# Two heads' rows of an attention output moved into the padding of the other heads, ahead of its output product

## The chip, the cores and the metric

The kernel runs on one core of one Trainium2 chip. A core has engines that run at the same time, each in the order of its own queue: TensorE (PE: matmuls, with the loading of weights beside them as PEld), VectorE (DVE), ScalarE (ACT), GpSimd (POOL) and SyncE (SP, which here only issues transfers). They wait for each other by semaphores. Transfers between the chip's memory (HBM) and the on-chip memory (SBUF) are issued from a queue (SP, POOL or ACT) and land later. Matmuls write to eight banks of accumulators, which ACT or DVE must read out before a bank can be used again. The metric is the device time of one execution in microseconds (us), the median over runs.

## The reference

x has 2048 rows of D = 448. It is normalized (xn); one branch is a local attention with 16 heads of 28 dimensions, the other an MLP with F = 1792; the result is x + s * g.

```python
def _A_ref(x, wqkv, wo):                   # H = 16, Dh = 28, W = 8, dil = 2
    qkv = (x @ wqkv).reshape(B, S, 3, H, Dh) ...
    q, k, v = qkv[0], qkv[1], qkv[2]
    idx = pos[:, None] - off[None, :]      # a row sees itself and 7 rows, 2 apart
    ...
    attn = _softmax(logits, axis=-1)
    o = jnp.einsum("bhsw,bhswd->bhsd", attn, vg)
    return o.transpose(0, 2, 1, 3).reshape(B, S, D) @ wo

def _B_ref(x, w1, b1, w2, b2):
    h = _gelu(jnp.einsum("bsd,df->bsf", x, w1) + b1)
    return jnp.einsum("bsf,fd->bsd", h, w2) + b2

xn = _layernorm(x)
s = _A_ref(xn, A_wqkv, A_wo)
g = _silu(_B_ref(xn, B_w1, B_b1, B_w2, B_b2))
return x + s * g
```

## The kernel before

**Tiles and stages.** The even rows of x come first and the odd rows after them, so that the 8 rows that a query sees lie next to each other. The 2048 rows are 16 tiles of 128 (index t), four tiles to a chunk of 512 (index c). Per tile: statistics and `norm` (line 482) make xn, which is turned into xnT (D on the partitions, four groups kt of 128; the fourth holds the last 64 dimensions twice, on partitions 0 to 63 and 64 to 127). `qk_rows` (589) and `vproj` (612) make q, k and v; q and k are turned by transposing transfers into qkT, v goes through a buffer in HBM, v_hbm, and comes back per visit. `ff1` (665, L671 and the gelu L675) and `ff2` (691, L703) are the MLP; `gate` (732) makes g from it. Attention runs in nine visits of 228 (one of 224) queries: the scores (L770), exp on ACT (L779), the mask on DVE (L785), the values (L799), and then four steps on DVE (L808 to L822) that divide by the sum and write oT. `final` (853) multiplies oT with wo (L863; L871 for the last two tiles), and `gated` (877) multiplies by g (sg), adds x (o) and stores.

**Row tiling.** D = 448 is three and a half times 128. `pair` (534) therefore takes two tiles of rows at once and splits every product in two halves of 64 rows, which run side by side on the array: first tile a on partitions 0 to 63 and tile b on 64 to 127, for the kt in `before`, and then, after a *hop*, the other way round for the kt in `after`. With xn, whose fourth kt is there twice, that is 4 + 3 steps, 14 matmuls a pair. The hop (`told`, 550 to 554) is a wait on POOL's queue: POOL waits until the last matmul of the first part is done and tells TensorE, which holds the second part until then. Other pairs' matmuls are placed in between. A change between 128-row, 64-row and 32-row matmuls is a change of mode.

**oT and wo.** A head has 28 dimensions, but oT gives it 32 partitions: head 4g + l lies on partitions 32g to 32g + 27 of kt = l. The four partitions that are left, 28 to 31, 60 to 63, 92 to 95 and 124 to 127 in each kt, hold what the division makes of the sums, and wo has zeros there (the memset at line 370). So the final product takes all four kt in both halves: 4 + 4 steps, 16 matmuls for each pair (line 865).

**The order.** The kernel writes out no order by hand. Each step is a task with an engine, an assumed duration, tasks that it needs, and a priority (PRIO, LATER, NUDGE); `_Plan.run` (102) places them one after the other in an assumed time and emits every engine's queue in that order. In it, a transfer issued from POOL is assumed to take 0.45 us of the queue (`dma`, 372). The queues then run as the chip lets them.

Of the kernel before, what the change touches and what calls it, by code (L numbers as in the profile page):

```python
# [8 lines left out]
F32 = mybir.dt.float32  # L9
BF16 = mybir.dt.bfloat16  # L10
# [7 lines left out]
TILED = 30  # L18
BURST = 3.5
NUDGE = {  # L20
    61: 4, 64: -20, 140: -165, 160: -221, 163: -244, 165: -29, 397: 111, 413: -37, 490: 163, 669: -149,
}
LAST = 352
SAME = 20
# [154 lines left out]
def kernel(  # L179
# [37 lines left out]
    def tok(ap):  # L217
        return ap.rearrange("b (s two) d -> two (b s) d", two=2)

    x_half = tok(A_x)  # L220
    o_half = tok(out)

# [8 lines left out]
    def sb(name, shape, dt=BF16):  # L231
        return const.tile(shape, dt, name=name)
# [6 lines left out]
    w1 = sb("w1", [P, KT, F])  # L239
    w2 = sb("w2", [P, NMT, D])  # L240
    wo = sb("wo", [P, KT, D])
    b1r = sb("b1r", [P, P])
    b1 = sb("b1", [P, NMT], F32)
    b2 = sb("b2", [P, D])
    xnT = sb("xnT", [P, KT, S])
    qkT = sb("qkT", [P, 2, G, PAD + S])
    v_tok = [sb(f"v_tok{t}", [P, 2, H // 2, 32]) for t in range(4)]
    v_hbm = dram.tile([BACK + S, H * 32], BF16, name="v_hbm")
    oT = sb("oT", [P, KT, S])
    ident = sb("ident", [P, P])  # L250
    eps_t = sb("eps_t", [P, 1], F32)
    half_t = sb("half_t", [P, 4], F32)
# [9 lines left out]
    def ring(name, n, shape, dt=BF16, fifo=False):  # L262
        return _Pool([sb(f"{name}{i}", shape, dt) for i in range(n)], fifo)

    p_xn = ring("xn", 4, [P, 512])
    p_st = ring("st", 4, [P, 6], F32)
    p_E = ring("E", 8, [P, 512], fifo=True)
    p_dt = ring("dt", 2, [P, 512], F32)
    p_rd = ring("rd", 2, [P, H], F32)
    p_y = ring("y", 2, [P, D], F32)  # L270
    p_t = ring("t", 2, [P, D], F32)
# [13 lines left out]


    PRIO = {
        "project": (54, 6.5, -1, -796,),
        "project2": (-47, -24.5, -697.5, -972,),
        "values": (-60, -238.5, -708, -812.5,),  # L290
        "attn": (332.5, 150, 124.5, 209.5, 61, 182.5, 339.5, 196.5, 276,),
        "ff1": (75, 107.5, 161, -24.5, -31, 92, 171.5, -1, -8, 117.5, 54, 79.5, 64, 6.5, 40, 96.5,
            13.5, 22.5, -0.5, 30, 190, 161.5, 181, 165.5, 181, 129, 104, 64.5,),
        "gelu": (-8, 79.5, 28, 194.5,),
        "ff2": (91.5, -34.5, -96.5, 114.5, 129.5, 89, -831.5, 135, 120, 180.5, 59, 104, 147.5, 131,
            -12.5, -48,),
        "final": (207.5, 2, 71.5, -16.5, 55.5, -2, 174.5, 203, 37, 65.5, -16, 162.5, 87.5, 134, 36,
            -5,),
        "norm": (131, 11, 219.5, 294, 62, 220, -31, 168.5, 7, 29.5, 162.5, 183.5, -110, 4.5, 164,
            134,),  # L300
        "loads": (227.5, 186, 183, 40, 129.5, 100, 27, -66,),
        "stats": (49, 32, 205.5, 205.5, 112, 82, 130.5, -5, 44.5, 27, 147.5, 207.5, 114, 203.5,
            217, 161,),
        "turn_x": (198, 4.5, 200, 12.5, 259, 121, 98.5, 186.5, 57, 57, 72, 135.5, 79, 58, 135, 88,),
        "turn_qk": (18.5, 126, 116, 140, -16, 32.5, 118.5, -91.5, 79.5, 15, 161.5, 121.5, 77.5,
            162.5, 166, -17.5,),
        "move_v": (129.5, 145.5, 200.5, 147.5, 126, 210.5, 218.5, 150, 100.5,),
        "store_v": (103, 80.5, 21.5, 52, 191, 92, 149, 31, 118, 150, 333.5, -0.5, 106, 223.5, 214,
            111,),
        "spread": (-10.5, 75.5, 298, 99.5, 52.5, 186.5, 149.5, -55, 104,),  # L310
        "copies": (187, 4, 219, 15.5, 90, 177, 88.5, 31, 29, 20.5, 182, 51, 204.5, 49.5, 24,),
    }
    LATER = {"swap": 191.5, "qk": 27, "v": 148, "gelu": 32.5, "exp": 149.5, "mask": -4394.5, "pv": -29.5, "recip": 100, "os": 224, "y": 202, "tanh": 79.5, "g": 204, "sg": 165.5, "o": 222.5}

    plan = _Plan()

    def buf(pool, owner, i=0):
        return pool.bufs[owner.slots[pool][i]]

    def pe(n, k=1):  # L320
        return k * (n / 2400.0 + 0.0025)
# [14 lines left out]
    def memset(eng, ap, v):  # L336
        def fn(_):
            getattr(nc, eng).memset(ap, v)
        return fn
# [27 lines left out]
    t_head = plan.add("POOL", 0.6, mk_head, [t_on], prio=91)  # L367
    t_row0 = plan.add("POOL", 0.1, memset("gpsimd", row0[:], 0.0), [t_on], prio=93)
    t_row0 = plan.add("POOL", 0.1, memset("gpsimd", row0[:1, :], 1.0), [t_row0], prio=93)
    t_wo = [plan.add("POOL", 1.6, memset("gpsimd", wo[:], 0.0), [t_ident], prio=98)]  # L370

    def dma(eng, dst, src, kb, prio, deps=(), issue=0.45, rate=350.0, tail=1.7, share=0):
        def fn(_):
            i = {"SP": nc.sync, "ACT": nc.scalar, "POOL": nc.gpsimd}[eng].dma_start(dst, src)
# [96 lines left out]
    def half_bank(ap):  # L471
        return ap[:].bitcast(BF16)[:, :512].rearrange("p (a b) -> p a b", a=4)
# [377 lines left out]
        return []  # L850


    def final(t, prio):
        if t >= NT - 2:
            for i, (cs, n, end) in enumerate(parts(t)):
                if i:
                    ff2_part(t, cs, n, end, PRIO["ff2"][t], [last])
                last = final_part(t, cs, n, t_g[t][i], prio - 0.1 * i)
        elif t % 2 == 0:
            def job(t):  # L860
                def part(ps, kt, half, start, stop):
                    r = half_rows(half)
                    return nc.tensor.matmul(ps[:, :D], oT[r, kt, t * P:(t + 1) * P], wo[r, kt, :], start=start, stop=stop)  # L863
                return _Job(D, part, t_oT[t] + t_wo + [t_f2[t]], lambda u, own, i: gated(t, slice(0, D), D, t_g[t][0], u, own, i, prio))
            pair(job(t), job(t + 1), prio, False, (range(KT),), (range(KT),))

    def final_part(t, cs, n, g, prio):
        def f1(k):
            ps = buf(p_b, k)
            for kt in range(KT):  # L870
                nc.tensor.matmul(ps[:, :n], oT[:, kt, t * P:(t + 1) * P], wo[:, kt, cs],  # L871
                                 start=(kt == 0), stop=(kt == KT - 1))
        a = plan.add("PE", pe(n, KT), f1, t_oT[t] + t_wo + [t_f2[t]], prio, take=(p_b,), tail=0.15)
        gated(t, cs, n, g, a, a, 0, prio)
        return a

# [88 lines left out]


    def f_b1(k):
        nc.tensor.transpose(half_bank(buf(p_b, k))[:, 0, :], b1r[:], ident[:])
    b1_at = plan.add("PE", 0.06, f_b1, [t_b1r, t_ident], 345, take=(p_b,), tail=0.15)
    t_b1 = plan.add("DVE", 0.17, lambda _: nc.vector.tensor_copy(b1[:], half_bank(buf(p_b, b1_at))[:, 0, :NMT]), [b1_at], 90,  # L970
                    give=((p_b, b1_at, 0),))

# [7 lines left out]
    for i, (lo, hi) in enumerate(((0, 4), (4, 7), (7, 11), (11, 14))):  # L980
        t_w2[i // 2].append(dma("SP", w2[:, lo:hi, :], B_w2[lo * P:hi * P, :].rearrange("(m p) c -> p m c", p=P),
                                112 * (hi - lo), PRIO["loads"][4 + i], first, rate=230.0, share=hi - lo))
    t_b2 = dma("POOL", b2[:], B_b2.rearrange("(o d) -> o d", o=1).to_broadcast((P, D)), 112, 82, turned)
    t_wo += [dma("POOL", wo[32 * g:32 * g + 28, :, :], A_wo[112 * g:112 * g + 112, :].rearrange("(l c) d -> c l d", l=4),
                 100, 80, [t_w2[1][0]] + t_wo[:1]) for g in range(G)]
    for t in range(2 * TPC, NT):
        stats(t)
        if t % TPC == TPC - 1:
# [8 lines left out]
    for i, (c, what) in enumerate(STAGES):  # L997
        if what == "A":
            if was == "F":
                exps = []  # L1000
            run += blocks_of[c]
            if i + 1 == len(STAGES) or STAGES[i + 1][1] != "A":
                state["gate"], state["early"] = gels, gels[:-1]
                for what, b in visits(run):
                    exps += attn(b, what)
                run = []
        else:
            if was == "A":
                gels = []
            hs = [ff1(c, mt, PRIO["gelu"][c], exps) for mt in range(NMT)]  # L1010
            for i in range(0, NMT, 2):
                ff1_last[c] = pair(hs[i], hs[i + 1], PRIO["ff1"][7 * c + i // 2], c < 2)
            gels = gels + [t_h[(c, mt)] for mt in range(NMT)]
            if c == 0:
                project(2)
                project(3)
            for t in range(c * TPC, (c + 1) * TPC):
                ff2(t, PRIO["ff2"][t])
        was = what
    for t in range(NT):  # L1020
        final(t, PRIO["final"][t])

# [33 lines left out]
```

## Time and profile before

| | |
|---|---|
| median of 3 runs (lowest, highest) | 152.42 us (152.16, 152.49) |
| profiled execution: its own time | 152.14 us |
| profiled execution: span of the core | 150.4 us |
| granted TensorE clock | 0.998 |
| transfers on SP's queue (q1) | 37790 packets, 17.84 MB |
| transfers on POOL's queue (q0) | 512 packets, 1.18 MB |

The span runs from the first to the last instruction of the core; the time holds what lies around it too. In the groups of the profile a line such as L863 is the line of the kernel; "64*128 64x448" is a matmul on 64 rows and 128 columns of the array with 448 columns of data; "x112 | 12.6, 349" are 112 instructions that are busy for 12.6 us together, 349 ns each, so that two of them overlap.

### The profile page before, as it was taken

What the parts mean: (1) busy time and instruction counts of PE and PEld (TensorE: products, weight loads), DVE (VectorE), ACT (ScalarE), POOL (GpSimd) and SP (SyncE); (2) the same over time, 40 slices, a digit from 0 to 9 for tenths busy, and PEclk for the clock granted to TensorE, in tenths of its full rate; (3) what the DMA queues carried; (4) which work ended last, traced back from release to release, by engine and by line L of the source; (5) the groups of instructions that cost most, each with busy time, mean ns of one, the idle gap of its engine ahead of it and who ended that gap; (6) DMA issues with size and microseconds to landing.
All of it is one profiled execution on the core that took longest, in us unless ns stands there. A gap on an engine that the chain in (4) does not pass through costs nothing.

```text
span 150.4 us, 5216 instructions
## 1 busy us (share of the span) xinstructions
PE 146.1 (97%) x2173; PEld 76.9 (51%) x2173; DVE 113.7 (76%) x276; ACT 96.0 (64%) x168; POOL 18.4 (12%) x51
## 2 busy tenths in 40 slices
PE   7999999999999999999999999999999999999990
PEld 2644444544455555558556554445556445555460
DVE  3876850495546889899997989497998978995962
ACT  3365877658496594785788648888567497822020
POOL 7425530201750000011000000000000000000000
PEclk9999999999999999999999999999999999999999
DMA  4999869889999957159967994521120000001212
GB/s 155 327 314 362 126 124 159 261 119 361 185 161 197 72 100 139 37 114 226 125 201 175 147 256 128 125 74 38 36 65 7 0 0 4 4 0 61 63 63 63
DMA packets 38470, 19.47 MB, mean 129 GB/s; under 512 B 24887, under 2 KB 37758, under 8 KB 38446
## 3 DMA queue, kind: packets, MB, share of 16 engines
q1 hardware_dynamic: 37790, 17.84, 53.9%
q0 software_dynamic: 512, 1.18, 4.5%
q8 instruction: 17, 0.28, 0.8%
q10 hardware_dynamic: 144, 0.11, 0.2%
q14 instruction: 7, 0.06, 0.1%
HBM read 9.42 MB, written 3.94 MB: 89 GB/s over the span
## 4 chain that ended last, share of the span: by engine, by line
PE 97%; DVE 0%; ACT 0%; issue 0%
PE bank L671 28%; PE bank L703 25%; PE bank L595 14%; PE bank L618 7%; PE bank L863 7%; PE bank L799 4%; PE bank L725 4%; PE bank L346 3%; PE bank L770 3%; PE bank L871 1%; PE bank L519 1%; DVE sg L883 0%; ACT w_in L744 0%; PE bank L503 0%; DVE o L890 0%; PE bank L723 0%
## 5 line engine op out<-in xcount | busy, mean ns | idle before, releaser
L671 PE MATMUL bank<-xnT,w 64*128 64x512 bf16 x392 | 44.1, 376 | 0.0
L675 ACT ACTIVATE h<-bank,b 128x512 bf16<-128x512 f32 x56 | 34.5, 687 | 11.7 <-PE bank L671 11.5
L703 PE MATMUL bank<-w,h 64*128 64x448 bf16 x392 | 40.2, 349 | 0.0
L671 PEld LDWEIGHTS <-w 64*128 64x128 bf16 x392 | 18.8, 94 | 22.1
L703 PEld LDWEIGHTS <-h 64*128 64x128 bf16 x392 | 18.6, 94 | 16.8
L595 PE MATMUL bank<-w_in,xnT 64*128 64x448 bf16 (+1 forms) x212 | 24.8, 350 | 0.0
L779 ACT ACTIVATE E<-bank 128x456 bf16<-128x456 f32 (+1 forms) x36 | 16.9, 554 | 9.9 <-PE bank L770 8.6
L331 ACT CAST qk_tok<-bank 128x448 bf16<-128x448 f32 x25 | 12.3, 539 | 5.9 <-PE bank L595 4.8
L595 PEld LDWEIGHTS <-xnT 64*128 64x128 bf16 (+1 forms) x212 | 10.8, 94 | 9.4 <-DVE xnT L333 0.2
L808 DVE STREAM_TRANSPOSE dt<-bank 128x480 f32<-128x480 f32 (+1 forms) x18 | 12.1, 673 | 4.5 <-PE bank L799 4.5
L618 PE MATMUL bank<-w_in,xnT 64*128 64x448 bf16 (+1 forms) x106 | 14.0, 350 | 0.0
L863 PE MATMUL bank<-wo,oT 64*128 64x448 bf16 x112 | 12.6, 349 | 0.0
L817 DVE STREAM_TRANSPOSE dt<-rd 128x480 f32<-128x480 f32 (+1 forms) x18 | 12.1, 675 | 0.6
L822 DVE TENSOR_TENSOR oT<-bank,dt 128x456 bf16<-128x456 f32 (+1 forms) x18 | 11.4, 632 | 0.6
L785 DVE TENSOR_TENSOR E<-E,m_gen 128x456 bf16<-128x456 bf16 (+1 forms) x32 | 10.8, 390 | 0.0
L443 DVE BATCH_NORM_STATS2 st<-x_sb 128x6 f32<-128x448 bf16 x16 | 9.5, 606 | 1.7 <-DMA x_sb<-in_A_x_dram 1.7
L333 DVE CAST qk_tok<-bank 128x448 bf16<-128x448 f32 x7 | 4.3, 620 | 8.6 <-PE bank L595 8.6
L737 DVE TENSOR_TENSOR y<-bank,b 128x448 f32<-128x448 f32 x15 | 8.7, 619 | 1.9 <-PE bank L703 1.8
L749 ACT ACTIVATE t<-y 128x448 f32<-128x448 f32 x12 | 6.7, 583 | 4.0 <-DVE y L737 4.0
L484 DVE TENSOR_SCALAR xn<-x_sb,mv,rstd 128x448 bf16<-128x448 bf16 x16 | 6.3, 393 | 3.6 <-POOL rstd L466 3.4
L744 ACT ACTIVATE w_in<-y 128x448 bf16<-128x448 f32 x3 | 1.7, 577 | 10.9 <-DVE y L737 10.9
L863 PEld LDWEIGHTS <-oT 64*128 64x128 bf16 x112 | 5.8, 94 | 4.8 <-issue 0.2
(76 smaller groups left out, 143.5 us busy)
## 6 DMA issues: line engine op xcount, KB each, us to landing
v<-v_hbm SPq DMA_DIRECT2D x16, 128.0 KB, 3.2
out_dram<-o SPq DMA_DIRECT2D x15, 112.0 KB, 2.0
v_hbm<-v_tok SPq DMA_DIRECT2D x13, 128.0 KB, 3.5
w<-in_B_w_dram SPq DMA_DIRECT2D x2, 672.0 KB, 6.7
w_in<-in_A_wqkv_dram SPq DMA_DIRECT2D x3, 336.0 KB, 4.2
x_sb<-in_A_x_dram SPq DMA_DIRECT2D x4, 224.0 KB, 4.1
w<-in_B_w_dram SPq DMA_DIRECT2D x2, 448.0 KB, 7.8
w<-in_B_w_dram SPq DMA_DIRECT2D x2, 336.0 KB, 8.9
```

What stands on the lines that cost most here:

```text
L331: nc.scalar.copy(o, i)
L595: return nc.tensor.matmul(ps[:, :D], xnT[r, kt, cs], w, start=start, stop=stop)
L618: return nc.tensor.matmul(ps[:, :D], xnT[r, kt, k0:k0 + P], w, start=start, stop=stop)
L671: return nc.tensor.matmul(ps[:], w1[r, kt, ms], xnT[r, kt, cs], start=start, stop=stop)
L675: nc.scalar.activation(buf(p_h, own, i)[:], buf(p_b, own, i)[:], ACT.Gelu_apprx_tanh, bias=b1[:, mt:mt + 1])
L703: return nc.tensor.matmul(ps[:, :D], buf(*h_at[(c, mt)])[r, cs], w2[r, mt, :], start=start, stop=stop)
L779: nc.scalar.activation(buf(p_E, k)[:, :8 * n], buf(p_b, a, at + i)[:, :8 * n], ACT.Exp, scale=SCALE)
L785: nc.vector.tensor_tensor(out=E, in0=E, in1=m[:, :, :, :n].rearrange("p i g q -> p (i g) q"), op=ALU.mult)
L808: nc.vector.transpose(buf(p_dt, k)[:, :32 * m], buf(p_b, po, i)[:, :32 * m])
L817: nc.vector.transpose(buf(p_dt, d)[:, :32 * m].rearrange("p (b c) -> p b c", c=32), buf(p_rd, r)[:, :m].unsqueeze(2).to_broadcast((P, m, 32)))
L822: nc.vector.tensor_tensor(out=oT[:, a::2, q:q + 4 * n1], in0=buf(p_b, po, i)[:, :n].rearrange("p (l q) -> p l q", l=2), in1=buf(p_dt, d)[: ...
L863: return nc.tensor.matmul(ps[:, :D], oT[r, kt, t * P:(t + 1) * P], wo[r, kt, :], start=start, stop=stop)
```

## The change

For the first three chunks the fourth kt of oT is cut from 128 partitions to 64. Its lower half, partitions 64 to 123, holds two heads (11 and 15) of 28 dimensions, 14 groups of four. `pack` moves these groups into spare partitions: one transfer stores the 60 partitions of the chunk to HBM (o_hbm), five transfers bring them back, four partitions each, as SPARE lists them, and two more copy partitions 0 to 63 of the fourth kt to 64 to 127 for the odd tiles. wo is laid out to match: four loads of 28 partitions, five of four partitions, and one copy from its upper to its lower half. `final` then calls `pair` with its usual 4 + 3 steps for tiles 0 to 11. The last chunk keeps the old layout, with a second weight tile, wo_all, which has the memset and four loads of its own.

oT becomes a view of the same tile as xnT: its first half is new, its columns from 1024 on lie over the columns of xnT that chunks 0 and 1 used. The tiles E and dt become shorter. The row of biases is turned as 64 partitions by 64 columns in 64-row mode, not 128 by 128. All priorities are new, and with them the order of every queue; what the new order does on TensorE is that all 128-row products of the first tiles come ahead of the first 64-row ones, and all products with wo come after the last FF1 of chunk 2.

```diff
+    SPARE = ((64, 28, 0, 4), (80, 60, 0, 3), (96, 60, 3, 1), (100, 92, 0, 3), (112, 124, 0, 3))
...
+    wo_all = sb("wo_all", [P, KT, D])
...
-    xnT = sb("xnT", [P, KT, S])
+    xT = sb("xT", [P, KT, HALF + S])
+    xnT, oT = xT[:, :, HALF:], xT[:, :, :S]
...
-    oT = sb("oT", [P, KT, S])
+    o_hbm = dram.tile([NCH - 1, 60, CH], BF16, name="o_hbm")
...
-    t_wo = [plan.add("POOL", 1.6, memset("gpsimd", wo[:], 0.0), [t_ident], prio=98)]
+    t_wo = []
+    t_wall = [plan.add("POOL", 1.6, memset("gpsimd", wo_all[:], 0.0), [t_ident], prio=98)]
...
+    def pack(c):
+        cs = slice(c * CH, (c + 1) * CH)
+        outs = [o for t in range(c * TPC, (c + 1) * TPC) for o in t_oT[t]]
+        a = plan.add("SP", 0.45, lambda _: nc.sync.dma_start(o_hbm[c, :, :], oT[64:124, 3, cs]), outs, PRIO["pack"][c])
+        away = plan.add("DMA", 0.2, lambda _: None, [a], 0, tail=2.0)
+        moved = []
+        for src, row, l0, n in SPARE:
+            def fn(_, src=src, row=row, l0=l0, n=n):
+                nc.sync.dma_start(oT[row:row + 4, l0:l0 + n, cs], o_hbm[c, src - 64:src - 64 + 4 * n, :].rearrange("(l j) q -> j l q", j=4))
+            a = plan.add("SP", 0.45, fn, [away], PRIO["pack"][c])
+            moved.append(plan.add("DMA", 0.1, lambda _: None, [a], 0, tail=2.2))
+        odd = [t for t in range(c * TPC + 1, (c + 1) * TPC, 2)]
+        for t in range(c * TPC, (c + 1) * TPC):
+            t_oT[t] = moved
+        for t in odd:
+            def fn(_, t=t):
+                nc.sync.dma_start(oT[64:, 3, t * P:(t + 1) * P], oT[:64, 3, t * P:(t + 1) * P])
+            a = plan.add("SP", 0.45, fn, moved, PRIO["pack"][c])
+            t_oT[t] = [plan.add("DMA", 0.1, lambda _: None, [a], 0, tail=2.0)]
...
+                w, loaded = (wo_all, t_wall) if t >= NT - TPC else (wo, t_wo)
...
-            pair(job(t), job(t + 1), prio, False, (range(KT),), (range(KT),))
+            if t >= NT - TPC:
+                pair(job(t), job(t + 1), prio, False, (range(KT),), (range(KT),))
+            else:
+                pair(job(t), job(t + 1), prio)
...
-        nc.tensor.transpose(half_bank(buf(p_b, k))[:, 0, :], b1r[:], ident[:])
-    b1_at = plan.add("PE", 0.06, f_b1, [t_b1r, t_ident], 345, take=(p_b,), tail=0.15)
+        nc.tensor.transpose(half_bank(buf(p_b, k))[:, 0, :64], b1r[:64, :], ident[:64, :64])
+    b1_at = plan.add("PE", 0.06, f_b1, [t_b1r, t_ident], 345, take=(p_b,), tail=0.15, mode=64)
...
-    t_wo += [dma("POOL", wo[32 * g:32 * g + 28, :, :], A_wo[112 * g:112 * g + 112, :].rearrange("(l c) d -> c l d", l=4),
-                 100, 80, [t_w2[1][0]] + t_wo[:1]) for g in range(G)]
+    for g in range(G):
+        n = KT if g < 2 else 3
+        t_wo.append(dma("POOL", wo[32 * g:32 * g + DH, :n, :], A_wo[112 * g:112 * g + DH * n, :].rearrange("(l c) d -> c l d", l=n), 25 * n, 80, [t_w2[1][0]]))
+    for src, row, l0, n in SPARE:
+        r0 = DH * (11 if src < 96 else 15) + src % 32
+        t_wo.append(dma("POOL", wo[row:row + 4, l0:l0 + n, :], A_wo[r0:r0 + 4 * n, :].rearrange("(l j) d -> j l d", j=4), 4 * n, 79, [t_w2[1][0]]))
+    t_wo.append(dma("POOL", wo[64:, 3, :], wo[:64, 3, :], 56, 78, list(t_wo)))
+    for g in range(G):
+        t_wall.append(dma("POOL", wo_all[32 * g:32 * g + DH, :, :], A_wo[112 * g:112 * g + 112, :].rearrange("(l c) d -> c l d", l=KT), 100, 77, [t_w2[1][0], t_wall[0]]))
...
+    for c in range(NCH - 1):
+        pack(c)
```

The new values of NUDGE, PRIO and LATER are left out. Once built, the changed program has 12 matmuls fewer on TensorE. POOL's queue holds 14 loads and copies of weights where it held four, and two stores of v that were on SP's; thirteen of the fourteen stand between the hops of FF1(1) and that of the first FF2 pair of chunk 0: one after the hop of the fourth pair of L671, five after that of the fifth, one after that of the sixth and six after that of the seventh. A transfer on POOL also waits until the one that used its semaphore before, eight transfers back, has landed.

More of the change, by code (lines that the diff above doesn't have):

```diff
@@ L20 @@
 NUDGE = {
-    61: 4, 64: -20, 140: -165, 160: -221, 163: -244, 165: -29, 397: 111, 413: -37, 490: 163, 669: -149,
+    154: 123, 160: 164, 258: -229, 325: 74, 329: 163, 523: 33,
 }
@@ L266 @@
     p_st = ring("st", 4, [P, 6], F32)
-    p_E = ring("E", 8, [P, 512], fifo=True)
-    p_dt = ring("dt", 2, [P, 512], F32)
+    p_E = ring("E", 8, [P, 8 * NW], fifo=True)
+    p_dt = ring("dt", 2, [P, 480], F32)
     p_rd = ring("rd", 2, [P, H], F32)
@@ L287 @@
     PRIO = {
[L288 to L310, printed above, removed]
+        "project": (74, 150.5, 63.5, -521.5,),
+        "project2": (50.5, -18, 466.5, -956,),
@@ new lines @@
+        "values": (-24, -308, 49.5, -775.5,),
+        "attn": (622.5, 183.5, 181.5, 141, 335.5, 53.5, 490.5, 118.5, 54.5,),
+        "ff1": (196, 214, 69, 54, 129.5, 171.5, 127, 105.5, 135.5, 147.5, 37, 63, 77.5, 117, 177.5,
+            40.5, -2.5, 176.5, 222, 118.5, 186, 81.5, -19.5, 3.5, 127.5, -293.5, 169.5, 154,),
+        "gelu": (176, 92.5, 138, 33.5,),
+        "ff2": (188, -34.5, 127, 114.5, -138.5, 89, -978, 135, 17, 180.5, 71, 104, 103.5, 131, -3,
+            -64,),
+        "final": (21.5, 2, 2, -16.5, 44.5, -2, -48, 203, 33, 65.5, 77, 162.5, 66, 134, 12.5, 184.5,),
@@ new lines @@
+        "norm": (131, 11, 219.5, 294, 48.5, 159, -4.5, 97, 73.5, 28, 161, 3, -147.5, 7, 88, 57,),
+        "pack": (77, 77, 41, 153.5,),
+        "loads": (43.5, -62.5, 186, 159.5, 66, 54, 113.5, 138,),
+        "stats": (49, 32, 205.5, 205.5, 83, 192.5, 121, 31, 48.5, 55.5, -7.5, 78.5, 124, 98.5, 60,
+            -34,),
+        "turn_x": (198, 4.5, 200, 12.5, 164.5, 35.5, 17.5, 50.5, -1.5, 23, 106.5, 8, 70, 199, 97,
+            38.5,),
+        "turn_qk": (111, 117.5, 67.5, 182.5, 4.5, 61.5, 135.5, -29, 69, 237.5, 161.5, 55, 186,
+            123.5, 209, 95,),
@@ L311 @@
+        "move_v": (137, 114, -12, 112.5, 4.5, 71, 115, 91, 27.5,),
+        "store_v": (15, 1, 298.5, 142.5, 109, 234, 251.5, 159.5, 63, 155.5, 123.5, 140.5, -23.5,
+            165.5, 217, 20.5,),
+        "spread": (-14, 104, 34.5, 28.5, -14, 211.5, -15, 78.5, 121,),
         "copies": (187, 4, 219, 15.5, 90, 177, 88.5, 31, 29, 20.5, 182, 51, 204.5, 49.5, 24,),
     }
-    LATER = {"swap": 191.5, "qk": 27, "v": 148, "gelu": 32.5, "exp": 149.5, "mask": -4394.5, "pv": -29.5, "recip": 100, "os": 224, "y": 202, "tanh": 79.5, "g": 204, "sg": 165.5, "o": 222.5}
+    LATER = {"swap": 1008.5, "qk": 68.5, "v": 212, "gelu": 15, "exp": 47, "mask": -42, "pv": 125.5, "recip": 135, "os": 194.5, "y": 135, "tanh": 57.5, "g": 120, "sg": 225, "o": 95.5}
@@ L860, in job @@
             def job(t):
+                w, loaded = (wo_all, t_wall) if t >= NT - TPC else (wo, t_wo)
                 def part(ps, kt, half, start, stop):
                     r = half_rows(half)
-                    return nc.tensor.matmul(ps[:, :D], oT[r, kt, t * P:(t + 1) * P], wo[r, kt, :], start=start, stop=stop)
-                return _Job(D, part, t_oT[t] + t_wo + [t_f2[t]], lambda u, own, i: gated(t, slice(0, D), D, t_g[t][0], u, own, i, prio))
-            pair(job(t), job(t + 1), prio, False, (range(KT),), (range(KT),))
+                    return nc.tensor.matmul(ps[:, :D], oT[r, kt, t * P:(t + 1) * P], w[r, kt, :], start=start, stop=stop)
+                return _Job(D, part, t_oT[t] + loaded + [t_f2[t]], lambda u, own, i: gated(t, slice(0, D), D, t_g[t][0], u, own, i, prio))
+            if t >= NT - TPC:
+                pair(job(t), job(t + 1), prio, False, (range(KT),), (range(KT),))
+            else:
+                pair(job(t), job(t + 1), prio)
     def final_part(t, cs, n, g, prio):
@@ L870, in f1 @@
             for kt in range(KT):
-                nc.tensor.matmul(ps[:, :n], oT[:, kt, t * P:(t + 1) * P], wo[:, kt, cs],
+                nc.tensor.matmul(ps[:, :n], oT[:, kt, t * P:(t + 1) * P], wo_all[:, kt, cs],
                                  start=(kt == 0), stop=(kt == KT - 1))
-        a = plan.add("PE", pe(n, KT), f1, t_oT[t] + t_wo + [t_f2[t]], prio, take=(p_b,), tail=0.15)
+        a = plan.add("PE", pe(n, KT), f1, t_oT[t] + t_wall + [t_f2[t]], prio, take=(p_b,), tail=0.15)
         gated(t, cs, n, g, a, a, 0, prio)
```

## The prediction

> **What bounds the kernel now.** First the page: the busy times and the chain of work that ended last.
>
> ```profile
> span 150.4 us, 5216 instructions
> ...
> PE 146.1 (97%) x2173; PEld 76.9 (51%) x2173; DVE 113.7 (76%) x276; ACT 96.0 (64%) x168; POOL 18.4 (12%) x51
> ...
> PEclk9999999999999999999999999999999999999999
> ...
> PE 97%; DVE 0%; ACT 0%; issue 0%
> ```
>
> TensorE is busy for 97% of the span, at full granted clock, and the chain is TensorE alone until the last stores. Since matmul ends are modelled, busy time by itself could hide waits, so next I read the chain in order of time (start, length, what):
>
> ```profile
> 9.39 0.30 PE bank L595 x2
> 9.69 0.19 PE bank L618 x2
> 9.88 0.16 PE bank L968
> 10.04 0.95 PE bank L595 x5
> 10.99 0.22 PE bank L503 x8
> 11.21 2.27 PE bank L595 x24
> 13.48 3.89 PE bank L671 x36
> ...
> 29.92 9.28 PE bank L671 x86
> ...
> 41.82 2.65 PE bank L703 x28
> 44.47 0.43 PE bank L770 x32
> ...
> 78.58 0.76 PE bank L863 x8
> ...
> 97.15 0.62 PE bank L799 x39
> ...
> 103.05 0.76 PE bank L671 x6
> 103.80 0.76 PE bank L863 x8
> ...
> 146.21 0.61 PE bank L725 x14
> ```
>
> The pieces abut and have one price per matmul from end to end: 9.28/86 = 0.108 us for L671, 2.65/28 = 0.0946 for L703, 0.76/8 = 0.0946 for L863 (two 64-row matmuls run at once). So TensorE never waits from 5.6 to 146.8 us. A matmul that goes is worth its price, and any wait that the new order brings is paid in full. The question is therefore whether the new order keeps TensorE supplied.
>
> **The change, part by part.**
>
> *The final product.* Six of the seven pairs of L863 lose one of their eight steps, two matmuls each: the diff goes from four kt after the hop to three.
>
> ```profile
> L863 PE MATMUL bank<-wo,oT 64*128 64x448 bf16 x112 | 12.6, 349 | 0.0
> ```
>
> From x112 it should go to x100: 12 x 0.0946 = **-1.13 us**. With TensorE always busy this is on the path; it would be less only where TensorE then waits for something else.
>
> *The bias turn.* Before, L968 runs in 128-row mode between 64-row work. Its 0.16 us, the 0.30 us of the first two 64-row L595 (0.19 without a change of mode) and the 0.22 us of L503 (whose eight 64-column matmuls are worth 0.11 by L671's rate per column) say that a change of row mode costs 0.11 us. In the new order all 128-row L595 and L618 stand ahead of the first 64-row matmul, so three changes become one: 0.11 + 0.11, and 0.03 for 64 columns in place of 128, **-0.24 us**; the bounds are 0 (TensorE meets a wait there, see below) and -0.25.
>
> *POOL.* This is where I expect the cost. Each row-tiled pair has its hop on POOL's queue (`told`, line 550): POOL must reach an instruction that waits for the first half before TensorE may start the second. Whatever POOL issues ahead of a hop can hold TensorE. The change takes POOL's weight loads from 4 to 14, and the new order puts two stores of v on it. What these cost, and how soon POOL starts after the matmul it waited for (start, duration, what, in brackets its wait):
>
> ```profile
> 11.67 0.23 POOL L954 TENSOR_SCALAR_AFFINE_SELECT m<-m 64x57 bf16<-64x57 bf16 x1
> 12.32 0.22 POOL L950 MEMSET m<- 128x57 bf16 x1 [0.41 <-PE bank L595]
> ...
> 14.10 0.24 POOL L956 TENSOR_SCALAR_AFFINE_SELECT m<-m 64x57 bf16<-64x57 bf16 x1
> ...
> 37.05 0.31 POOL L465 TENSOR_SCALAR sd<-mv,eps_t 128x4 f32<-128x4 f32 x1 [6.90 <-PE bank L671]
> 37.44 1.04 POOL L466 TENSOR_TENSOR rstd<-sd,half_t 128x4 f32<-128x4 f32 x1
> ...
> 40.82 2.46 POOL L374 DMA_DIRECT2D wo<-in_A_wo_dram  x4
> ```
>
> The same by line (duration of one issue in ns, minimum/median/maximum; then issue to landing in us):
>
> ```profile
> L389 POOL DMA_DIRECT2D v_hbm<-v_tok x3: 555/575/588, 28.6 to 68.0; - x3
> ...
> L374 POOL DMA_DIRECT2D wo<-in_A_wo_dram x4: 586/596/702, 40.8 to 42.7; - x4
> ...
> DMA to landing us min/median/max: 3.5/4.5/5.4
> ```
>
> (a) *Two v stores* now stand between the first hop and the seven mask instructions (12.32 to 14.34, 2.02 us). The first mask ends at 11.90; 11.90 + 2 x 0.575 + 2.02 = 15.07, plus hops about 15.15. L671 starts 8 L595 and 0.24 us earlier than 13.48, at 12.48, and its first second half is due 24 matmuls on, at 15.07. **+0.15**, bounds 0 and 0.3.
>
> (b) *Five loads between two hops of FF1(1).* The block of 98 L671 still starts near 29.92. POOL's hop before them fires after matmul 58, at 36.18; the lag to POOL is 0.22 (in the old program the hop ahead of 37.05 follows matmul 64, at 36.83), so 36.40. The second half behind the next hop is due after matmul 86, at 39.20. That leaves 2.80 us for five issues: 2.46/4 = 0.615 each makes 3.07, so 0.27 late; with the way back to TensorE **+0.3**. Bounds: 0.555 each makes 2.78, no stall; 0.702 makes 3.51, 0.75. No load with a 4-row target is in the trace; the nearest rows are these, and a v store of 128 KB (0.575) costs what a wo load of 98 KB does (0.596), so size tells little.
>
> (c) *Six loads ahead of the hop in FF2(0).* One load and a hop later POOL is at 40.1; six issues of 0.6 end at 43.7. That hop is due when 98 L671, 28 L703 and 32 L770 are done: 40.49 + 2.65 + 0.43 + 0.3 = 43.87. But the last four also wait until a load issued between 36.4 and 38.3 has landed (their semaphores are reused in turn). With 4.5 us the last could start at 42.8, no wait; with 5.4 at 43.7, ending 44.3. **+0.1**, bounds 0 and 0.45.
>
> The Trainium skill ("DMA: Bandwidth & Descriptors", section "Anatomy of one DMA — SWDGE (gpsimd) path") gives such a transfer about 50 ns of dispatch, a small variable cost to generate descriptors, and about 2.0 us fixed. By that page (b) and (c) would be nothing and the time 151.2; the rows above, 0.6 us an issue and 4.5 us to land, disagree, and the sum keeps to them.
>
> *SP.* Twenty-four new transfers, eight a chunk: one store, five loads, two copies. Behind chunk 0's wait stand the last two qkT transposes, two loads of v for visit 5 and half of visit 4's; behind chunk 2's the output stores, which hold the `o` ring of DVE. Nearest rows (KB, us to landing):
>
> ```profile
> v<-v_hbm SPq DMA_DIRECT2D x16, 128.0 KB, 3.2
> out_dram<-o SPq DMA_DIRECT2D x15, 112.0 KB, 2.0
> v_hbm<-v_tok SPq DMA_DIRECT2D x13, 128.0 KB, 3.5
> ```
>
> The tightest user is the second pair of L863, tiles 4 and 5. FF1(2) ends at 103.80; with three pairs of L863 (48 x 0.0946 = 4.54) moved behind it, at 99.3. Then come 14 L863, 112 L703, three score visits, one value visit and 8 L671, 14.8 us: due 114.1. Visit 4's values end at 97.78 - 4.54 + 0.65 (six more L671 ahead) = 93.9. DVE needs 4.5 us for a visit:
>
> ```profile
> 114.81 0.68 DVE L808 STREAM_TRANSPOSE dt<-bank 128x480 f32<-128x480 f32 x1 [0.48 <-PE bank L799]
> ...
> 118.78 0.63 DVE L822 TENSOR_TENSOR oT<-bank,dt 128x456 bf16<-128x456 f32 x1
> 119.33 0.61 DVE L753 SCALAR_TENSOR_TENSOR g<-t,y 128x448 bf16<-128x448 f32 x1
> ```
>
> So the store goes at 98.4, and three landings of 2.0 to 3.5 with some 4 us of issues end at 108.5 to 113. The cover is 1 to 5.6 us: **0**, bounds 0 and 1. Chunk 0 has over ten us, chunk 2 about six. Half of visit 4's v is issued behind chunk 0's loads: by the same prices visit 2's values end at 74.9 in the new order, its output at 79.4, and a landing, some 5 us of issues and the 3.2 make 90 to 91; it is due at 93.2.
>
> *The rest.* oT over the columns of xnT: these were last read by FF1(1), done at 40.5, and are written after 93.9: 0. The memset of the second wo only moves on POOL, ahead of hops: 0. Three pairs of L863 moved later bring their sg and o to DVE after 99 us:
>
> ```profile
> L885 DVE SCALAR_TENSOR_TENSOR sg<-bank,g 128x448 bf16<-128x448 f32 x10 | 6.2, 620 | 1.3 <-ACT E L779 0.9 <-PE bank L863 0.3
> ...
> L890 DVE TENSOR_TENSOR o<-x_sb,sg 128x448 bf16<-128x448 bf16 x15 | 5.9, 391 | 1.4 <-DMA out_dram<-o 0.9
> ```
>
> 3 x 2 x (0.62 + 0.39) = 6.1 us. Walking DVE's new order there with the durations above, the banks of L671 come free 0.6 to 1.4 us before they are due: 0, bounds 0 and 0.4.
>
> *Sum.* -1.13 - 0.24 + 0.15 + 0.3 + 0.1 = -0.8 us. The profiled execution took 152.14 us (span 150.4 and 1.74 around it), 0.28 under the median 152.42. So 151.3 for it, and on the median 151.6; for small waits in the tight order that I can't place I add 0.1: **151.7 us**.
>
> **The rivals.**
>
> 1. *No wait at all.* Loads of few rows issue faster than any row here, and only the removed work shows: 152.42 - 1.37 = 151.05. For it: the margins missed in (a) and (b) are 0.1 to 0.3 us. Against: five issues fit 2.80 us only at the lowest duration in the trace.
>
> 2. *Slower: POOL waits for landings.* One mechanism, the hop in (c): if the loads between 36.4 and 38.3 take L to land, TensorE waits L - 5.0. The gain is used up at L = 5.9. With L = 7.0, the median of the w loads below, the wait is 2.0 and the time 152.42 - 1.37 + 0.45 + 2.0 = 153.5. For it: more loads are in flight, and xnT transposes run beside them. Against: four loads beside such transposes landed within 5.4.
>
> ```profile
> L374 SPq DMA_DIRECT2D w<-in_B_w_dram x10: 374/576/1802, 5.0 to 31.5; - x10
> ...
> DMA to landing us min/median/max: 5.6/7.0/8.9
> ```
>
> 3. *The gain is given back.* The packing chain of chunk 1 or DVE in the dense stretch after 99 us ends late by 0.7 to 0.9: 152.4. For it: DVE has little to spare,
>
> ```profile
> 110.00:120.00 10.00, 10.00 (x218) 5.57 (x216) 9.28 (x22) 6.05 (x12) 0.00 (x0) 1.00 0.06 16
> ```
>
> (9.28 of 10 us); against: the old order at the same load never made TensorE wait. The Trainium skill ("DMA: Bandwidth & Descriptors", section "Rules for kernel authors") says to coalesce small transfers, since under 64 KB one pays mostly overhead; all 24 are below that. No row here has such a transfer into four rows.
>
> That the change does not do what it says I give no weight: twelve matmuls are gone from the new order.
>
> **How the numbers follow.** Forecast 0.58, no wait 0.13, slower 0.15, given back 0.14. The forecast's own range is 151.1 to 152.2, from the bounds of (a) to (c). For 8 in 10 the range must take in rival 1 and part of rival 2: 150.8 to 153.2. A difference of 0.2%, 0.3 us, is about what this kernel's runs can tell from none. Faster than 152.1: all of rival 1, nearly all of the forecast: 0.69. Within 0.3 us: most of rival 3 and an edge of the forecast: 0.13. Slower: 0.18.
>
> **What would show it.** L863 with x100 in the 64-row form and 0.0946 us a matmul; L968 as 128x64 with no mode changes around it; the chain's L671 piece from 29.9 longer than 98 x 0.108 = 10.58 by 0.2 to 0.7, with POOL's loads ending between 39.2 and 39.9; L703 behind the first L770 starting late by under 0.5; nothing but TensorE on the chain after 50 us. It is wrong if L671 has no excess near 39 us, if TensorE waits over 1 us behind POOL near 44, or if a wait on xT or on a bank appears after 99 us.

## The result, and the profile after

The changed kernel took 153.13 us (median of 14 runs, 152.54 to 155.73) against 152.37 (151.70 to 152.91) for the kernel before: a ratio of 1.0054, 95% interval 1.0032 to 1.0075. It is slower, by some 0.8 us. The prediction was 151.7 us and faster; the time lies just inside its range (150.8 to 153.2), on the wrong side of no change. A second set of runs (a0_after, below) gave 1.0018 (0.9991 to 1.0045): there it is not told from no change, and not faster either. The ratios leave out the executions in the chip's slow state, here one of the 14 (155.73 us).

The page of the changed kernel, with its span, busy times, chain and the group of the final product:

```profile
span 151.1 us, 5239 instructions
...
PE 145.7 (96%) x2161; PEld 78.2 (52%) x2161; DVE 116.3 (77%) x282; ACT 91.8 (61%) x162; POOL 26.2 (17%) x64
...
PE 86%; DMA 6%; SPq 4%; issue 1%; POOL 1%; DVE 0%; ACT 0%; POOLq 0%
...
L889 PE MATMUL bank<-wo,xT 64*128 64x448 bf16 x84 | 10.0, 349 | 0.0
```

The twelve matmuls are gone (2173 to 2161; 84 of the product with wo and 16 with wo_all make the forecast 100; L863 is L889 now). But the span grew from 150.4 to 151.1 us, and the chain of work, 97% TensorE before, now holds 6% of transfers and 4% of SP. TensorE waits. The waits of TensorE, grouped (what it waited for: us in total, times, longest), name the larger part:

```profile
PE bank L803 <- DMA v<-v_hbm: 1.4, 2, 0.8
```

L803 are the values of a visit (L799 before). The chain in order of time shows where, and a third place on POOL (start, length, what):

```profile
11.82 0.12 PE bank L507 x8
11.94 0.03 PE bank L997
11.97 0.71 PE bank L599 x6
12.68 2.69 PE bank L675 x24
15.37 0.09 POOL m L985
15.46 0.05 issue
15.51 2.12 PE bank L675 x18
17.62 0.76 PE bank L599 x8
...
30.29 10.58 PE bank L675 x98
...
68.42 0.61 POOL v L393
69.04 6.36 DMA v<-v_hbm
75.39 0.04 issue
75.44 0.69 PE bank L803 x39
...
89.80 1.99 SPq L865
...
92.51 2.62 DMA v<-v_hbm
95.13 0.04 issue
95.18 0.69 PE bank L803 x39
```

- *Near 12 us.* The turn of the biases costs what was forecast (L507 0.12 and L997 0.03, no change of mode), but six L599 take 0.71 where 6 x 0.0946 = 0.57 is due: they are the part behind the first hop, which is no longer covered. +0.14.
- *Near 15 us.* 42 L675 are worth 42 x 0.108 = 4.54 and should end at 17.22; they end at 17.62, behind a mask on POOL. +0.40.
- *Near 75 us.* Visit 2's values wait for their second load of v, which POOL issued at 69.04, behind the first (68.42), and which landed 6.36 us later. +0.8.
- *Near 95 us.* Visit 4's values wait for the second half of their v, which SP issued after chunk 0's five packing loads (L865), one of which took 1.99 us to issue. +0.6.
- The block of 98 L675 at 30.29 is 98 x 0.108 = 10.58, to the hundredth. Where steps (b) and (c) put their stalls there is none.

-1.13 - 0.24 + 0.14 + 0.40 + 1.4 = +0.6, against the +0.7 of the spans. So the gain is there, and four waits give back more than it. The two large ones lie between 66 and 100 us; the stretch in both kernels, before first (core's stretch: length, then busy times of PE, PEld, DVE, ACT and POOL, granted clock, share of the DMA engines, GB/s):

```profile
66.00:100.00 34.00, 34.00 (x602) 19.10 (x600) 29.26 (x64) 25.26 (x47) 1.14 (x2) 1.00 0.79 165
```

```profile
66.00:100.00 34.00, 32.65 (x638) 17.40 (x635) 27.88 (x60) 26.16 (x49) 1.84 (x3) 1.00 0.90 154
```

TensorE loses 34.00 - 32.65 = 1.35 us in this stretch alone, at full clock. The share of the DMA engines goes from 0.79 to 0.90, but that isn't shown to be the cause: in the same view e10_pack_only (below) has a share of 0.71, and its TensorE is busy for 32.55 us.

### The profile page after: what moved, and what is told of

It is laid out like the page before. It is cut to its first block, busy times and chain, and to the rows that moved or that the text cites. A ratio compares the mean times of both kernels' runs of the same rounds, so it can differ in the third digit from the quotient of the medians.

```text
span 151.1 us, 5239 instructions
## 1 busy us (share of the span) xinstructions
PE 145.7 (96%) x2161; PEld 78.2 (52%) x2161; DVE 116.3 (77%) x282; ACT 91.8 (61%) x162; POOL 26.2 (17%) x64
## 4 chain that ended last, share of the span: by engine, by line
PE 86%; DMA 6%; SPq 4%; issue 1%; POOL 1%; DVE 0%; ACT 0%; POOLq 0%
PE bank L675 24%; PE bank L707 23%; PE bank L599 12%; PE bank L889 6%; DMA v<-v_hbm 6%; PE bank L622 5%; PE bank L803 4%; PE bank L729 4%; PE bank L349 3%; SPq L865 2%; PE bank L774 2%; SPq L393 1%; PE bank L900 1%; SPq L401 1%; PE bank L523 1%
## 5 line engine op out<-in xcount | busy, mean ns | idle before, releaser
L675 PE MATMUL bank<-xT,w 64*128 64x512 bf16 x392 | 44.8, 376 | 0.1
L675 PEld LDWEIGHTS <-w 64*128 64x128 bf16 x392 | 18.9, 94 | 22.4 <-POOLq L555 0.6
L707 PEld LDWEIGHTS <-h 64*128 64x128 bf16 x392 | 19.8, 94 | 15.4
L599 PE MATMUL bank<-w_in,xT 64*128 64x448 bf16 (+1 forms) x212 | 24.6, 350 | 0.0
L334 ACT CAST qk_tok<-bank 128x448 bf16<-128x448 f32 x21 | 10.8, 536 | 10.7 <-issue 4.7
L599 PEld LDWEIGHTS <-xT 64*128 64x128 bf16 (+1 forms) x212 | 10.6, 94 | 10.2 <-issue 0.6
L336 DVE CAST qk_tok<-bank 128x448 bf16<-128x448 f32 x11 | 6.7, 622 | 8.5 <-PE bank L599 8.5
L622 PE MATMUL bank<-w_in,xT 64*128 64x448 bf16 (+1 forms) x106 | 12.7, 349 | 0.0
L826 DVE TENSOR_TENSOR xT<-bank,dt 128x456 bf16<-128x456 f32 (+1 forms) x18 | 11.4, 632 | 0.6
L889 PE MATMUL bank<-wo,xT 64*128 64x448 bf16 x84 | 10.0, 349 | 0.0
L334 ACT CAST v_tok<-bank 128x448 bf16<-128x448 f32 x12 | 6.2, 535 | 4.8 <-PE bank L622 4.5
L803 PE MATMUL bank<-E,v 64*32 64x57 bf16 (+1 forms) x576 | 6.7, 190 | 1.4 <-DMA v<-v_hbm 1.4
```

The lines of the kernel that those rows point to most:

```text
L334: nc.scalar.copy(o, i)
L599: return nc.tensor.matmul(ps[:, :D], xnT[r, kt, cs], w, start=start, stop=stop)
L622: return nc.tensor.matmul(ps[:, :D], xnT[r, kt, k0:k0 + P], w, start=start, stop=stop)
L675: return nc.tensor.matmul(ps[:], w1[r, kt, ms], xnT[r, kt, cs], start=start, stop=stop)
L707: return nc.tensor.matmul(ps[:, :D], buf(*h_at[(c, mt)])[r, cs], w2[r, mt, :], start=start, stop=stop)
L803: nc.tensor.matmul(banks[a][32 * g:32 * g + 32, c0:c0 + n], buf(*v_at[b])[r, s, 2 * g + h, :], buf(p_E, exps[2 * h + s // 2])[r, c1:c1 + n ...
```

## The experiments

All keep the changed kernel's order on TensorE instruction for instruction unless said otherwise. The plan is left as it is; unless said otherwise, only the queue or the place at which a few transfers are issued is changed. Ratios are to the kernel before, timed in the same rounds (its median was 152.1 to 152.2 us in the three sets; e9_seven_loads, e10_pack_only, e11_v2_only and a0_after ran on another chip than the rest of the experiments). The diffs are in outline.

**Each wait taken away alone, and all three.** In e1_v2_sp visit 2's loads of v go to SP; in e3_store_sp the v stores of tiles 0 and 1 do; in e2_pack_late chunk 0's packing loads are issued behind the second half of visit 4's v. e4_all has all three.

```diff
     def dma_sb(dst, src, deps, prio, take=(), late=False, sp=False):
         def fn(k):
-            (nc.gpsimd if k.on == "POOL" else nc.sync).dma_start(dst(k), src())
+            (nc.gpsimd if k.on == "POOL" and not sp else nc.sync).dma_start(dst(k), src())
...
 # e1: loads of v       sp = (b == 2)
 # e3: stores of v      sp = (t < 2)
 # e2: after the plan, the loads of pack(0)
+    a.start = max(a.start, half_v[4].start + 0.01)
```

> The order of the changed kernel with one thing different: the two loads of v for visit 2 are issued on SP's queue, between its qkT transposes, not on POOL's. Theory (three separate waits: POOL's masks near 15 us 0.4, visit 2's v 0.9, visit 4's v 0.6): the wait ahead of visit 2's values (start 75.44, due 74.5) goes, 0.8 to 0.9 us less, 152.3; visit 4's wait stays, smaller by what SP runs earlier. Rival (the transfers are crowded at that time, whichever queue issues them): v lands after 74.5 all the same and less than 0.3 us is gained, 152.9 or more. Second rival: SP's queue gets 1.3 us longer there, and a later transpose or load is late in its place.

> The order of the changed kernel with one thing different: on SP, the second half of visit 4's v goes ahead of the five loads of chunk 0's packing, not behind them. Theory: that load is issued near 89 instead of 92.5 and has landed by 93, so the wait ahead of visit 4's values (start 95.18, due 94.5) goes: 0.6 us less, 152.5; visit 2's wait stays. Rival (the load is late because v_hbm's rows or the buffer come late, not because of the queue): no gain, 153.1.

> The order of the changed kernel with one thing different: the stores of v for tiles 0 and 1 are issued on SP, as before the change, not on POOL ahead of the masks. Theory: the hop behind the masks is met near 14.3 instead of 15.5, L675's break at 15.3 us goes, the block of 98 L675 starts at 29.9 instead of 30.3: 0.4 us less, 152.7. Rival (TensorE meets the next thing that is late, such as w1 or a gelu): the block of 98 starts later than 30.1 and less than 0.2 us is gained.

> The three edits together. Theory: the waits are separate and add up, 0.4 + 0.9 + 0.6 = 1.9 us less than the changed kernel, 151.2, some 1.1 us under the kernel before; the chain is TensorE from 5.6 us to the end. Rival (there is slack elsewhere that then runs out, DVE or the banks): under 1.2 us of it is gained, 151.9 or more.

| | median, us | ratio (95%) |
|---|---|---|
| changed kernel | 153.13 | 1.0054 (1.0032 to 1.0075) |
| e1_v2_sp | 152.58 | 1.0015 (0.9990 to 1.0040) |
| e2_pack_late | 152.19 | 0.9993 (0.9970 to 1.0017) |
| e3_store_sp | 152.70 | 1.0014 (0.9983 to 1.0044) |
| e4_all | 151.05 | 0.9925 (0.9901 to 0.9948) |

Against the changed kernel's 1.0054 each repair gives back some 0.6 to 0.9 us, uncertain by some 0.5, and together they give back 0.0129 x 152.4 = 2.0 us. Against a0_after's 1.0018 e1_v2_sp and e3_store_sp would give back under 0.1 us, and e2_pack_late 0.4, so these three runs don't settle the single shares. The losses that stay vary too: in e1_v2_sp's profile visit 4's v costs 0.8 us, and in e2_pack_late's, which has no wait for v near 95 us, TensorE stands still for 0.88 us near 76 us. e4_all (6 runs, where the others have 10 to 12) is faster than both kernels, with nothing left out. Its waits of TensorE have no entry but the one at the start of the program, and its chain reads as the one of before did:

```profile
12.46 4.62 PE bank L678 x42
17.08 0.76 PE bank L599 x8
...
29.74 10.58 PE bank L678 x98
...
73.97 0.63 PE bank L806 x40
74.59 2.75 PE bank L622 x28
...
93.00 0.62 PE bank L806 x39
93.62 3.99 PE bank L678 x36
```

(L678 and L806 are L675 and L803 here, three lines lower.) The 42 matmuls near 12 are one piece, and both value visits follow the matmul ahead of them.

**One wait left in.** The other way round: from e4_all one repair is taken back. In e6_stores_only the two stores are on POOL again, in e10_pack_only the packing loads are ahead again, in e11_v2_only visit 2's loads are on POOL again. a0_after is the changed kernel once more, timed with the last two.

> e4_all with one of its three repairs taken back: the v stores of tiles 0 and 1 stand on POOL again, between the two sets of masks, as in the changed kernel. Theory: 42 L675 again come in two pieces with the second mask set between them, TensorE waits 0.4 us near 15 us, and nothing else changes: 0.4 us over e4_all, 0.995 of before. Rival (the stores cost by the load that they put on the DMA engines early, or the wait is made up later): under 0.15 us over e4_all. A second rival, read from the spread of the three single repairs: 0.6 us or more, by landings that come later as well.

> The changed kernel with two of the three repairs (v stores of tiles 0 and 1, and visit 2's v loads, on SP): chunk 0's five packing loads still stand on SP ahead of the second half of visit 4's v. Theory: only the wait of the values of visit 4 is left, near 94 us, 0.6 us (0.3 to 0.9), so 0.9925 + 0.004 = 0.9965 of before. Rival (the packing loads were late for it only because everything before was late): under 0.2 us over e4_all.

> The changed kernel with the other two repairs (v stores of tiles 0 and 1 on SP, chunk 0's packing loads behind visit 4's v): visit 2's v loads stay on POOL. Theory: only the wait of the values of visit 2 is left, near 74 us, 0 to 0.9 us, as these loads take 4.4 to 6.4 us to land (due about 5.4 us after the second issue), so the runs spread more than those of e4_all, about 0.995 of before. Rival (POOL's loads land no later than SP's, the wait in the changed kernel was one run's): e4_all's time and spread.

> The changed kernel as it is, on the chip of the next runs, so that what the single repairs give back is compared on one chip. Theory: 1.0054 of the kernel before again (1.003 to 1.008), 2.0 us over e4_all, which is the sum of the three waits (0.4, 0.85 and 0.6).

| | median, us | ratio (95%) | over e4_all, us |
|---|---|---|---|
| e6_stores_only | 151.54 | 0.9958 (0.9946 to 0.9971) | 0.50 |
| e10_pack_only | 152.48 | 0.9997 (0.9964 to 1.0030) | 1.10 |
| e11_v2_only | 152.12 | 0.9992 (0.9962 to 1.0021) | 1.02 |
| a0_after | 152.73 | 1.0018 (0.9991 to 1.0045) | 1.41 |

(The last column is the difference of the ratios times 152.1; it is uncertain by some 0.4 to 0.6.) Each cause alone makes the kernel slower than e4_all. The stores cost about what the trace showed; the packing loads (0.3 to 0.9 expected) and visit 2's loads (0 to 0.9 expected) cost more than expected. e10's chain says why the packing's size varies:

```profile
87.17 2.80 SPq L401
...
91.91 2.63 DMA v<-v_hbm
94.55 0.04 issue
94.59 0.68 PE bank L803 x39
```

Here it isn't a packing load but the transpose issued ahead of them that took long, 2.80 us (1.28 in the changed kernel's profile), and the values came 1.6 us after e4_all's 93.00. The five loads stand between it and v either way.

e11's runs go from 151.03 to 152.96 us, those of e4_all from 150.62 to 151.55. Its profile, of a run of 151.78 us, has visit 2's values in time (74.01): there TensorE loses some 0.6 us near 80 to 81 us, where visit 3's scores and values wait, the latter for a cast on DVE. So that run's loss isn't the wait that was expected. Five profiles have visit 2's loads on POOL. The second load landed 4.0, 5.0, 5.4, 5.6 and 6.4 us after its issue, with some 5.4 us of room: the values waited for 0.2 us at 5.6 and for 0.8 at 6.4, and not at all in the other three. That the slower runs of e11 are those with the late landing would fit, but isn't shown.

a0_after, with all three causes, is below the sum of the three and below its expected 1.0054. In its profile visit 2's v is in time and visit 4's wait is 0.3; why its runs lose less isn't shown.

**The product undone.** e4_all with the main part of the change taken out: all products by wo_all with four kt after the hop, and no packing transfers.

```diff
-                pair(job(t), job(t + 1), prio)
+                pair(job(t), job(t + 1), prio, full=True)   # range(KT) in both parts, wo_all
```

> e4_all with the change's main part undone: the six pairs of the first three chunks multiply all four kt after the hop, against the zero-padded weights as before, and none of the 24 packing transfers is issued; every other instruction keeps its place. L889's twelve matmuls come back (x84 to x96 in the 64-row form). Theory (the product's saving is paid out in full once TensorE meets no wait): 12 x 0.0946 = 1.13 us over e4_all, so about 1.000 of the kernel before, some 152.2 us on the chip of e4_all. Rival (the packing transfers themselves take something back by their load on the DMA engines and on SP): less than 0.7 us over e4_all.

152.07 us, 1.0004 (0.9985 to 1.0023): 0.0079 x 152.1 = 1.20 us over e4_all, where 1.13 was expected. The saved matmuls are on the path and are paid out in full; the 24 small transfers take nothing measurable from it (the difference is uncertain by some 0.5) once they stand in the right place. The rule of the Trainium skill ("DMA: Bandwidth & Descriptors", section "Rules for kernel authors") that small transfers should be coalesced didn't decide this case: where they stood in SP's queue did.

**What holds a hop.** Step (b) of the prediction let a hop wait for every issue ahead of it on POOL, and the profile after shows no stall there. I first took it that queued issues don't hold a hop at all, and only instructions that wait on one another, as the masks do, hold it. e7_eight_loads puts eight loads of wo between two hops of FF1(1) in place of five; e8_op_behind_loads leaves five and puts two masks behind them.

```diff
 # e7 (e9: two loads), in the order on POOL
-  hop, 5 loads, hop, load, hop, 2 loads, 4 loads of wo_all
+  hop, 8 loads, hop, hop, 4 loads of wo_all
 # e8
-  hop, 5 loads, hop
+  hop, 5 loads, affine_select(m1), affine_select(m1), hop
```

> e4_all with three more of POOL's wo loads moved ahead of the hop inside FF1(1), so that eight stand between two hops in place of five. In e4_all these eight were issued from 36.62 to 41.36 us, and the second half behind the hop is due after 86 of 98 L675, at 29.74 + 86 x 0.108 = 39.0. Prediction's step (b) (a hop waits until the issues ahead of it are done): TensorE would wait until 41.4, 2.3 us more than e4_all, in the middle of the block of 98 L675. Theory now (POOL's sequencer passes the issues on and goes ahead, so the hop fires when TensorE reaches it): no wait, the block stays 98 x 0.108 = 10.58 us, and the time stays e4_all's within 0.2 us.

> e4_all with one addition: behind the five wo loads and ahead of the same hop inside FF1(1), POOL gets two more mask instructions on an old mask tile that nobody reads any more, the second of which waits for the first. Theory (the hop itself isn't held by queued issues, but by an instruction ahead of it that waits for another of POOL, and that one stands behind the issues): five issues from 36.62 end at 39.6, the first instruction ends near 39.85, the hop fires near 40, and TensorE, due at 39.0, waits 0.8 to 1.2 us: about 1.0 us over e4_all. Prediction's step (b): five issues alone would already have cost 0.5 us in e4_all, which its trace doesn't show; with the two instructions 1.0 us. Rival (a hop is never held by work in POOL's queue): no wait, e4_all's time.

e7 took 152.32 us, 1.0018 (0.9998 to 1.0037), 1.4 over e4_all: both the theory's 0 and step (b)'s 2.3 are wrong. Its chain:

```profile
29.62 6.27 PE bank L678 x58
...
36.50 3.60 POOL wo L378 x7
40.10 0.05 issue
40.14 1.47 PE bank L678 x12
41.61 2.65 PE bank L710 x28
```

The eight issues take 4.74 us, 0.593 each, and would end at 41.24. The hop passed at 40.1, when 3.60/0.593 = 6.1 of them were done: it stood two issues ahead of the work. From this a third theory, for e9_seven_loads:

> e7_eight_loads with seven loads between the two hops in place of eight. In e7 the hop passed at 40.1 us, six issues of 0.593 after their start at 36.50: two loads ahead of it were still to be done. Theory (POOL's queue holds two issues behind which the sequencer may already stand, and no more): with seven the hop passes after five, at 36.5 + 5 x 0.593 + 0.05 = 39.5, TensorE is due at 38.9, waits 0.6, and the time is 0.6 to 0.8 us over e4_all. Rival (in e7 the eighth load waited until the first one, issued at 35.1, had landed, since their semaphores are reused in turn): without the eighth there is no wait, and the time is e4_all's. Prediction's step (b) (the hop waits for all issues ahead of it): 36.5 + 7 x 0.593 = 40.65, 1.7 us over e4_all.

```profile
30.02 6.27 PE bank L678 x58
...
36.89 3.06 POOL wo L378 x6
39.95 0.05 issue
40.00 1.47 PE bank L678 x12
```

3.06/0.593 = 5.2 issues, of seven: again two fewer. TensorE was due at 30.02 + 86 x 0.108 = 39.31 and went on at 40.00; the wait of 0.7 was expected as 0.6, and the time, 152.14 us, 0.9993 (0.9974 to 1.0012), is 1.0 over e4_all, a little above the 0.6 to 0.8. The rival with the reused semaphore falls, and so does step (b)'s 1.7. With the changed kernel's five loads the hop is free after three, at 37.17 + 3 x 0.593 = 38.95, and TensorE needs it at 39.58: no wait.

e8 took 152.49 us, 1.0025 (1.0007 to 1.0044), 1.5 over e4_all, where about 1.0 was expected; the wait in its profile is the expected one:

```profile
36.83 2.99 POOL wo L378 x5
39.81 0.01 issue
39.83 0.25 POOL m L1071
40.08 0.04 issue
40.12 0.03 POOLq L555
40.15 0.05 issue
40.19 1.47 PE bank L678 x12
```

All five issues and the first of the two masks were done (40.08) before the hop passed (40.12), since the second mask waits for the first; the second itself didn't hold it. So the masks near 15 us do hold their hop, until the last of them starts (15.37, TensorE at 15.51). Whether one instruction that waits for nothing would hold it as well was not run.

## Why the prediction was wrong, by its steps

- *Product, -1.13:* right. The trace has x84 and x16, and e5_product_undone gives 1.20.
- *Turn of the biases, -0.24:* right in itself; 0.14 of it is lost at the first hop, in e4_all too. That the two changes of mode had covered this hop before is argued, not shown. The bounds (0 to -0.25) held it.
- *(a) The stores on POOL, +0.15:* right in mechanism, mis-sized: 0.40 in the trace, 0.50 by e6_stores_only. The step counted the stores from the end of the first set of masks; POOL stood still ahead of them. From the view of POOL's work in order of time:

```profile
12.45 1.16 POOL L393 DMA_DIRECT2D v_hbm<-v_tok  x2 [0.48 <-ACT qk_tok L334]
13.65 0.15 POOL L979 MEMSET m<- 128x57 bf16 x1
...
15.37 0.24 POOL L985 TENSOR_SCALAR_AFFINE_SELECT m<-m 64x57 bf16<-64x57 bf16 x1
```

  The 0.48 us before them, in which POOL waited for ACT, were not in the sum. (The view names the cast of qk_tok that follows the cast of v on ACT; which of the two the store needs isn't shown.)
- *(b) and (c) The loads of wo between hops, +0.3 and +0.1:* wrong. The durations were right (0.593 us each). The five issues of (b) began at 37.17, counted from the start of the block 0.4 later than forecast, and took until 40.14 (5 x 0.593); by the step's rule TensorE, due at 39.58, would have waited some 0.6. The six of (c) ended at 44.27, and TensorE went on behind that hop at 43.94. Neither waited: a hop doesn't wait for the last two issues ahead of it (e7, e9), and so both came to 0. Rival 2, which put its stall in (c), fell with them.
- *SP, "0, bounds 0 and 1":* a step that failed: it put this wait at nothing. It had visit 4's v at "90 to 91; due 93.2"; it landed at 95.13. The sum had a landing and some 5 us of issues between visit 2's output, at 79.4, and the load of v. SP's queue, in order of time:

```profile
82.68 0.40 SPq L860 DMA_DIRECT2D o_hbm<-xT  x1
83.18 2.26 SPq L401 DMA_TRANSPOSE qkT<-qk_tok  x1
85.55 1.29 SPq L393 DMA_DIRECT2D v<-v_hbm  x2
86.89 0.60 SPq L393 DMA_DIRECT2D v_hbm<-v_tok  x1
87.60 1.28 SPq L401 DMA_TRANSPOSE qkT<-qk_tok  x1
88.97 3.50 SPq L865 DMA_DIRECT2D xT<-o_hbm  x5
```

  Chunk 0's packing store goes at 82.68, and from there to the load of v at 92.51 the issues take 9.8 us, almost without a gap, the five loads 3.50 of them. The 5 us of issues are the term that was mis-sized, about twofold. The cost is 0.6 in the trace, 0.3 to 1.5 over the profiles that have this wait, 1.1 by e10_pack_only. Chunks 1 and 2 were in time, as said: no wait after 100 us.
- *Not in the sum at all: visit 2's v.* The new order gives these two loads to POOL; before, they were on SP. The prediction looked at what POOL's issues do to hops and forgot what POOL's queue does to the user of the data. 0.8 in the trace; 1.0 by e11_v2_only, though that run's profile shows no such wait. In the changed kernel's profile this alone is as large as the gain of 0.7 that was forecast.

Rival 3 (given back, 152.4) came nearest to the outcome, but named another place: the dense stretch after 99 us, where the trace shows TensorE without a wait. That the range held the time is luck: its upper end stood there for rival 2, whose stall didn't come.

Three things stay open. In two profiles with visit 2's v on POOL (e2_pack_late and a0_after) TensorE stood still for 0.88 and 0.46 us right after those values, with no wait that the profile shows; e4_all has nothing there. How much of e11_v2_only's 1.0 us is the wait for visit 2's v isn't known. And a0_after's smaller loss wasn't traced to one of the waits.

## What to carry to other kernels

Where an order is new, list every transfer that changed its queue or its neighbours ahead in the queue, and compare its landing with the time at which its user is due; looking at the engines that issue them isn't enough. A saving on an engine that never waits is worth its full price only while every feed of it stays ahead: here nine transfers in three wrong places (two stores, two loads of v, five packing loads) cost 2.0 us, more than the 1.2 that the change brings, and moving them, with TensorE's order untouched, made the version that beats both kernels (151.05 us, 0.9925). Count every issue that stands ahead in the queue: here 5 us of issues were counted and 9.8 passed, and a landing that was put at 90 to 91 us came at 95.13.

## What was not expected of the hardware

- An instruction on POOL's queue that only waits for TensorE and tells it passes while two transfers ahead of it are still to be issued: after 6.1 of 8 and 5.2 of 7 issues. Two instructions of which the second waits for the first take that lead away (40.12 in e8_op_behind_loads, behind 2.99 us of issues and 0.25 of the first).
- Issues on SP that mostly take 0.3 us (loads of four partitions) or 1.3 us (transposes) took up to 1.99 in the changed kernel and 2.80 in e10_pack_only. A fuller set of DMA engines isn't shown to be the reason: from 66 to 100 us their share was 0.90 in the first and 0.71 in the second, and the kernel before has a transpose of 2.84 us too.
- A load of v of 128 KB took 6.36 us to land when issued from POOL near 69 us, and another of the same size 2.62 from SP near 92 us, in one execution. The load from POOL took 4.0 to 6.4 us over five profiles.
